# The tail of a fused attention and spectral-mixing kernel: order, PSUM banks and pieces of the last rows

## The chip, the cores and the metric

The kernel runs on one NeuronCore of a Trainium2 chip. The metric is device time in microseconds from one execution, and a kernel's time is the median of its runs; less is better. Before the change three runs gave 427.49, 428.01 and 428.20 us, so the median is 428.01 us.

A core has five engines with instruction streams of their own: TensorE (PE in the profile; its weight loads are listed as PEld), VectorE (DVE), ScalarE (ACT), GpSimd (POOL) and SyncE (SP). They meet only through semaphores. Sixteen DMA engines move data between HBM and SBUF; SP, ACT and POOL each put transfers into a queue of their own. TensorE writes its results to PSUM, which has 8 banks of 512 float32 columns by 128 partitions. ACT and DVE read PSUM and write SBUF.

## The reference

Inputs q, k, v have the shape (8, 8, 576, 64): batch, heads, sequence, head width. Four heads attend to the last 32 positions and four to positions at a stride of 32. The result is laid out as x with shape (8, 576, 512). Then a spectral layer follows:

```
X = rfft(x, axis=1)[:, :64]                 # 64 modes
Yr = Xr @ w_r - Xi @ w_i                    # per mode: 512 x 512 matrices
Yi = Xr @ w_i + Xi @ w_r
u  = x + irfft(Y)                           # Y is zero above mode 63
out = u + max(u @ w_ch, 0)                  # w_ch is 512 x 512; out is (8, 576, 512) float32
```

The weights w_r and w_i are 64 x 512 x 512 float32 each (134 MB together) and are read once. The output is 9.44 MB.

## The kernel before

The work runs in stages: attention per batch; a discrete Fourier transform by matmul; the products with the mode weights; and the way back. A mode's weights are loaded in two halves of the 512 input channels (`ORDER`), by POOL, which casts them to float16 on the way. The load order sets the order of the modes. The last to come are modes 48 to 63 of half 0, which are slot 1 of the function `mode`; the very last four are loaded one mode at a time, real and imaginary part in a DMA each (line 190).

`mode(1, m)` for these modes multiplies with the weights as the stationary operand: 16 matmuls of 16 columns (line 630). Eight modes share one PSUM bank `y`. `spectrum` (DVE, line 563) then adds the half that was computed before and writes the whole spectrum `YT`. For modes 56 to 63 it is called twice, after mode 61 for six modes and after mode 63 for two.

The inverse transform of 64 modes is split in groups of 16 modes. The sum is linear, so the kernel also carries u @ w_ch through the spectrum: z = Y @ w_ch per mode (`spec_z`, line 736, four matmuls accumulating over channels), and y turned by four transposes. The first three groups are added early (`renew`) to `v0` (rows of x @ w_ch) and `xo` (rows of x), both kept in float16. The last group, modes 48 to 63, is the tail's work. z and y of it come in two halves of the batch: `zzs[0]`, `yys[0]` for batches 0 to 3, `zzs[1]`, `yys[1]` for batches 4 to 7.

The tail has 18 items. An item is a pair of batches and one of four row blocks of 128 rows (items 0 to 15, of which 0 to 7 are batches 0 to 3), or four batches and their last 64 rows (items 16 and 17, t = 4). For each item k:

- `v_early(k)` puts v0 into a PSUM pair of two banks (two matmuls of 512 columns with an identity, line 987). `new_rows(k, v, zzs)` adds the last group (two to four matmuls with 32 rows, line 1001). `v_done(k)` is the relu on ACT (line 1013).
- `u_early(k)` and `new_rows(k, u, yys)` do the same with xo (lines 992, 1001). `u_done(k)` adds u and the relu on DVE into `osb` (line 1020), and SP issues the store (line 1028). For t = 4 the store goes as four DMAs of 64 rows (line 1031), two from SP and two from ACT; batches of even number lie on partitions 0 to 63, those of odd number on 64 to 127.

`pieces(k)` says whether ACT, DVE and the store take an item whole or as two batches after each other.

The order of instructions on each engine is the order in which the Python program issues them (`manual_schedule`), and each engine works it off in order. Tile pools hand out buffers and put in the waits that reuse needs. In the tail, PSUM pool `p` has three pairs, pool `y` two single banks; after the last mode `y` is closed, its two banks become `zp` and `yp` (pool `s`), and after that the one pair `u`. Whoever takes `u` first must wait until both `zp` and `yp` have been read.

Before the change the sequence is: modes 56 to 61 with `renew` between them; mode 62; `v_early(0)`, `v_early(1)`, `u_early(0)`; mode 63; z of the first half; one copy by ACT; eight transposes for both halves of y; two copies by DVE; items 0 and 1; then a loop in which v of item k and u of item k - 1 go side by side. z of the second half is computed at k = 8, in a bank of pool `p`:

```
        if k == 8:
            held = psum("p", pair=True)[:, 0]
            spec_z(3, 1, held)
            act_copy(zzs[1], held)
```

Of the kernel before, what the change touches and what calls it, by code (L numbers as in the profile page):

```python
# [10 lines left out]
FP = mybir.dt.float32  # L11
# [8 lines left out]
NM = 64  # L20
# [36 lines left out]
def kernel(  # L57
# [10 lines left out]
    nc = tc.nc  # L68
# [6 lines left out]
    pss = {}  # L75
# [10 lines left out]
    def psum(kind, half=False, pair=False):  # L86
        if pair:
            return pss[kind].tile([128, 2, 512], FP, tag=kind, name=kind)
        if half:
            return pss[kind].tile([128, 1024], F16, tag=kind, name=kind)  # L90
        return pss[kind].tile([128, 512], FP, tag=kind, name=kind)
# [28 lines left out]
    YS = {}  # L120
# [33 lines left out]
    w_chs = {}  # L154
# [95 lines left out]
    def act_copy(out, in_):  # L250
        nc.scalar.activation(out=out, in_=in_, func=ACTF.Copy)  # L251
# [303 lines left out]
    def flush():  # L555
        while queued:
            queued.pop()()
# [56 lines left out]
    def mode(slot, m):  # L614
        half = 1 - slot
        if m % 2:
            flush()
        if slot == 0 or m < SPLIT0:
            if m % 2:
                mode_pair(slot, m - 1)  # L620
            return
        mi, mg = m % 8, m // 8
        if mi == 0:
            ypt[slot] = psum("y")
        yp = ypt[slot]
        yv = yp.rearrange("p (m e x) -> p m e x", m=8, e=4)
        wt = w_tiles[ORDER.index((half, m))]
        for e in range(4):
            for c in range(4):
                nc.tensor.matmul(  # L630
                    yv[:, mi, e, :],
                    wt[:, XC[c], ds(128 * e, 128)],
                    Xh[half][:, c, :, :, m],
                    start=(c == 0),
                    stop=(c == 3),
                )
        if m % 2:
            w_fetch()
        ends = {5: 6, 7: 2} if mg == 7 else {7: 8}
        if mi in ends:  # L640
            n = ends[mi]
            m0 = mi + 1 - n
            spectrum(
                slot,
                (slice(None), slice(None), mg // 2, slice(None), ds(8 * (mg % 2) + m0, n)),
                yp.rearrange("p (m e x) -> p e x m", m=8, e=4)[:, :, :, ds(m0, n)],
            )
# [85 lines left out]
    def spec_z(g, bq, zp):  # L733
        for e in range(4):
            lhs = YS["YT"][:, e, g, ds(8 * bq, 8), :].rearrange("p x m -> p (x m)")
            nc.tensor.matmul(
                zp, lhs, w_chs["n"][:, e, :], start=(e == 0), stop=(e == 3)
            )
# [102 lines left out]
    for b in range(B):  # L841
# [12 lines left out]
        n = 0  # L854
        nm = NMODES[b]
        for mi in range(nm):
# [3 lines left out]
            n = upto  # L860
# [8 lines left out]
    zzs = [ptr.tile([128, DM], F16, name=f"zz{i}") for i in range(B)]  # L869
    yys = [ptr.tile([128, DM], F16, name=f"yy{i}") for i in range(B)]  # L870
# [56 lines left out]
    n = 0  # L927
    for m in range(SPLIT0):
# [4 lines left out]
        n = upto  # L933
# [33 lines left out]
    for n, i in enumerate([3, 5, 7] + list(range(8, 21))):  # L967
        b, t = n // 2, n % 2 * 2
# [8 lines left out]
    LAST = len(items) - 1  # L977
    vps, ups, rls, osbs = {}, {}, {}, {}
# [3 lines left out]
        return [kept[b][:, t] for b in bs] if t < 4 else [half[b // 2] for b in bs[::2]]  # L982

    def v_early(k):
        vps[k] = psum("p", pair=True)
        for j, r in enumerate(own(items[k], v0s, v0h)):
            nc.tensor.matmul(vps[k][:, j], idn, r, start=True, stop=False)  # L987

    def u_early(k):
        ups[k] = psum(("p", "u")[k % 2], pair=True)  # L990
        for j, r in enumerate(own(items[k], xos, xoh)):
            nc.tensor.matmul(ups[k][:, j], idn, r, start=True, stop=False)

    def new_rows(k, acc, spectra):
        bs, t = items[k]
        for j, b in enumerate(bs):
            q = ds(32 * (b % 4), 32)
            o, cols = acc[:, j % 2], out_cols(t)
            if t == 4:
                o = acc[ds(64 * (b % 2), 64), j // 2]  # L1000
            nc.tensor.matmul(  # L1001
                o, A3[q, cols], spectra[b // 4][q], start=False, stop=True
            )

    def pieces(k):
        return [slice(0, 1), slice(1, 2)] if k == 0 else [slice(0, 2)]

    def v_done(k):
        rl = ptr.tile([128, 2, 576], FP, tag=("xT", "rl")[k // 2 % 2], bufs=2, name="rl")
        rls[k] = rl[:, :, 0:DM]  # L1010
        vp = vps.pop(k)
        for j in pieces(k):
            nc.scalar.activation(out=rls[k][:, j], in_=vp[:, j], func=ACTF.Relu)  # L1013

    def u_done(k):
        bs, t = items[k]
        up, rl = ups.pop(k), rls.pop(k)
        osb = pw.tile([128, 2, DM], FP, tag="w", name="osb")
        for j in pieces(k):
            nc.vector.tensor_tensor(  # L1020
                out=osb[:, j], in0=up[:, j], in1=rl[:, j], op=AluOp.add
            )
            if t < 4:
                rows = out[:, ds(128 * (t - t % 2), 256), :].rearrange(
                    "b (p i) e -> p b i e", i=2
                )
                own_b = slice(bs[0] + j.start, bs[0] + j.stop)
                nc.sync.dma_start(rows[:, own_b, t % 2], osb[:, j])
        if t == 4:
            for b in bs:  # L1030
                (nc.scalar if b % 2 else nc.sync).dma_start(
                    out[b, ds(512, 64), :], osb[ds(64 * (b % 2), 64), b // 2 % 2, :]
                )

    flush()
# [5 lines left out]
            w()  # L1041
    yctx.close()
    with tc.tile_pool(name="ps_s", bufs=1, space=PSUM) as pss["s"]:
        zp = pss["s"].tile([128, 512], FP, name="zp")
        yp = pss["s"].tile([128, 2, 512], F16, name="yp")
        spec_z(3, 0, zp)
        act_copy(zzs[0], zp)
        for bq in range(2):
            for e in range(4):
                lhs = YS["YT"][:, e, 3, ds(8 * bq, 8), :].rearrange("p x m -> p (x m)")  # L1050
                nc.tensor.transpose(yp[:, bq, ds(128 * e, 128)], lhs, idn)
        for bq in range(2):
            nc.vector.tensor_copy(out=yys[bq], in_=yp[:, bq])
    pss["u"] = pctx.enter_context(tc.tile_pool(name="ps_u", bufs=1, space=PSUM))

    for k in range(2):
        new_rows(k, vps[k], zzs)
    for k in range(2):
        v_done(k)
    for k in range(2):  # L1060
        if k:
            u_early(k)
        new_rows(k, ups[k], yys)
        u_done(k)
    for k in range(2, LAST + 2):
        if k == 8:
            held = psum("p", pair=True)[:, 0]
            spec_z(3, 1, held)
            act_copy(zzs[1], held)
        if k <= LAST:  # L1070
            v_early(k)
        if k > 2:
            u_early(k - 1)
        if k <= LAST:
            new_rows(k, vps[k], zzs)
        if k > 2:
            new_rows(k - 1, ups[k - 1], yys)
        if k <= LAST:
            v_done(k)
        if k > 2:  # L1080
            u_done(k - 1)
    psum_pools()


# [28 lines left out]
```

## Time and profile before

The page does not give the profiled execution's whole time; its span is 426.7 us, 1.3 us under the median of the three runs.

| What | Value |
|---|---|
| Median of three runs | 428.01 us |
| Span of the profiled execution | 426.7 us |
| PE, DVE, ACT busy | 346.4, 234.7, 218.3 us |
| Last weight DMA issued, time to its landing | 382.31 us, 9.6 us |
| First store issued | 396.88 us |
| Stores of items 0 to 15 | 17 DMAs, 343 to 392 ns of SP each, 2.1 to 3.8 us to landing |
| Stores of items 16 and 17 | 8 DMAs of 128 KB, 528 to 846 ns of the issuer each, 2.4 to 3.4 us to landing |
| DMA share, 410.2 to 420.0 us | 1.02, 379 GB/s |

How to read it: a row of the timeline has the start, the duration, engine, line, operation and tiles, and in brackets the idle time of the engine before it and what ended it. A row of the windows has, for a stretch of time, each engine's busy time, the granted clock of TensorE as a share of full speed, the mean busy share of the 16 DMA engines and what they moved. A share slightly over 1 comes from packets that overlap.

### The profile page before, as it was taken

The numbers are of one execution on the slowest core, as the hardware profiler recorded it, in microseconds if no ns is written. First come the engines' busy times: TensorE is split into PE (matmuls) and PEld (weight loads), VectorE is DVE, ScalarE is ACT, GpSimd is POOL, SyncE is SP. The second block draws the span as 40 slices with busy tenths as digits, with TensorE's granted clock in tenths as the row PEclk, the third lists the DMA queues.
The fourth block names the chain that finished last, engine by engine and source line by source line (L and its number), as shares of the span: only waits on it lengthen the run. The fifth ranks groups of instructions, "written<-read, shape, count | busy, mean of one in ns | idle before, by whom it ended". The sixth has DMA issues, their size and how long they took to land.

```text
span 426.7 us, 9768 instructions
## 1 busy us (share of the span) xinstructions
PE 346.4 (81%) x4167; PEld 208.2 (49%) x4167; DVE 234.7 (55%) x466; ACT 218.3 (51%) x390; POOL 110.7 (26%) x196
## 2 busy tenths in 40 slices
PE   2977878769999698889768788878788867889993
PEld 2866767554656365566433344435444423445330
DVE  3788778851355154356113246746676354655884
ACT  1687678643656356556642235423442444443872
POOL 8332333322423222222222322222232222210000
PEclk9999899967999689999995889989999979989997
DMA  8999999999999999999999999999999999995698
GB/s 150 210 212 212 213 213 213 211 211 211 214 213 213 213 213 215 212 214 215 210 214 211 213 214 213 210 213 215 212 213 214 213 213 214 214 212 105 244 355 287
DMA packets 30938, 91.62 MB, mean 215 GB/s; under 512 B 4464, under 2 KB 5232, under 8 KB 30896
## 3 DMA queue, kind: packets, MB, share of 16 engines
q0 software_dynamic: 25168, 81.28, 96.2%
q1 hardware_dynamic: 4976, 9.13, 5.9%
q10 hardware_dynamic: 752, 0.61, 0.5%
q8 instruction: 32, 0.52, 0.5%
q14 instruction: 10, 0.08, 0.0%
HBM read 162.83 MB, written 9.44 MB: 404 GB/s over the span
## 4 chain that ended last, share of the span: by engine, by line
DMA 47%; PE 29%; DVE 14%; ACT 5%; issue 3%; DVEq 0%; POOL 0%; ACTq 0%; POOLq 0%
DMA wt<-in_moe_w_i_dram 38%; DMA wt<-in_moe_w_r_dram 7%; PE y L597 5%; DVE xb L241 3%; DVE kz L283 3%; PE p L987 2%; ACT X L251 2%; PE sc L532 2%; PE tp L413 2%; PE sc L459 1%; PE p L1001 1%; PE y L532 1%; PE p L760 1%; DVE yy L752 1%; DVE rec L240 1%
## 5 line engine op out<-in xcount | busy, mean ns | idle before, releaser
L597 PE MATMUL y<-wt,X 128*32 128x512 f16 (+1 forms) x448 | 70.9, 430 | 20.1 <-DMA wt<-in_moe_w_i_dram 20.1
L186 POOL DMA_DIRECT2D wt<-in_moe_w_r_dram x59 | 34.7, 588 | 126.4 <-PE y L597 56.3
L186 POOL DMA_DIRECT2D wt<-in_moe_w_i_dram x60 | 35.4, 590 | 68.3 <-DMA wt<-in_moe_w_i_dram 44.4
L597 PEld LDWEIGHTS <-X 128*32 128x32 f16 (+1 forms) x448 | 28.1, 140 | 39.4 <-DMA wt<-in_moe_w_i_dram 18.6
L727 DVE COPY xo<-tp 128x512 f16<-128x512 f16 x32 | 22.1, 691 | 36.8 <-PE tp L725 36.8
L726 ACT ACTIVATE v<-sc 128x512 f16<-128x512 f32 x32 | 19.1, 597 | 44.2 <-PE sc L717 44.2
L717 PE MATMUL sc<-w_cp,xT 128*128 128x512 f16 x128 | 36.9, 410 | 1.9 <-DVE xT L690 1.9
L489 ACT ACTIVATE PL<-sc 128x480 f16<-128x480 f32 (+1 forms) x48 | 27.0, 578 | 21.3 <-PE sc L475 21.0
L241 DVE TENSOR_TENSOR xb<-av,rec 90x256 f16<-90x256 f32 (+2 forms) x80 | 36.0, 450 | 2.8
L240 DVE RECIPROCAL rec<-av 90x4 f32<-90x4 f32 (+2 forms) x80 | 14.6, 183 | 39.3 <-PE av L504 28.2
L251 ACT ACTIVATE yr<-y 128x512 f16<-128x512 f32 x28 | 16.7, 597 | 36.8 <-PE y L597 35.6
L961 DVE TENSOR_TENSOR xo<-p,xo 128x1024 f16<-128x1024 f32 x16 | 19.6, 1225 | 21.7 <-PE p L760 21.7
L420 DVE COPY qT<-tp 128x576 f16<-128x576 f16 x16 | 11.9, 752 | 34.7 <-PE tp L413 34.7
L251 ACT ACTIVATE v<-p 128x1024 f16<-128x1024 f32 x16 | 16.4, 1023 | 23.1 <-PE p L760 23.1
L378 ACT ACTIVATE PL<-sc 90x360 f16<-90x360 f32 (+1 forms) x48 | 22.7, 490 | 7.0 <-PE sc L371 6.4
L251 ACT ACTIVATE v<-tp 128x640 f16<-128x640 f16 (+1 forms) x24 | 19.0, 807 | 11.8 <-PE tp L447 9.3
L413 PE MATMUL tp<-cI_s,ring 64*64 64x64 f16 x864 | 22.4, 197 | 2.7 <-DVE qT L420 2.4
L459 PE MATMUL sc<-cMl_s,cI_s 128*128 128x480 f16 (+1 forms) x48 | 19.4, 405 | 4.5 <-ACT PL L489 2.9
L276 PE MATMUL tp<-cI_s,ring 72*128 72x72 f16 x256 | 15.4, 207 | 8.7 <-DMA ring<-in_v_dram 7.1
L413 PEld LDWEIGHTS <-ring 64*64 64x64 f16 x864 | 17.5, 110 | 9.4 <-issue 5.4
L251 ACT ACTIVATE kz<-tp 64x360 f16<-64x360 f16 (+1 forms) x32 | 18.9, 592 | 6.2 <-PE tp L413 5.2
L1013 ACT ACTIVATE rl<-p 128x1024 f32<-128x1024 f32 (+1 forms) x19 | 18.4, 979 | 5.7 <-PE p L1001 3.1
(142 smaller groups left out, 737.9 us busy)
## 6 DMA issues: line engine op xcount, KB each, us to landing
wt<-in_moe_w_i_dram POOLq DMA_DIRECT2D x60, 512.0 KB, 18.8
wt<-in_moe_w_r_dram POOLq DMA_DIRECT2D x59, 512.0 KB, 17.7
out_dram<-osb SPq DMA_DIRECT2D x15, 512.0 KB, 3.4
ring<-in_v_dram POOLq DMA_DIRECT2D x8, 288.0 KB, 13.4
ring<-in_q_dram POOLq DMA_DIRECT2D x8, 288.0 KB, 13.6
ring<-in_k_dram POOLq DMA_DIRECT2D x8, 288.0 KB, 13.1
ring<-in_v_dram POOLq DMA_DIRECT2D x3, 512.0 KB, 14.8
ring<-in_q_dram POOLq DMA_DIRECT2D x3, 512.0 KB, 14.8
```

Of the source, the lines that this page charges most:

```text
L186: nc.gpsimd.dma_start(dst, rows)
L241: nc.vector.tensor_tensor(out=dst, in0=val.rearrange("p h (q c) -> p h c q", c=4), in1=rec[0:n, 0:pieces] .to_broadcast((n, pieces, 64)) . ...
L251: nc.scalar.activation(out=out, in_=in_, func=ACTF.Copy)
L378: nc.scalar.activation(out=PS[0:n, ds(POFF[t], 4 * n)], in_=scp[0:n, 0 : 4 * n], func=ACTF.Exp, scale=SCALE,)
L413: nc.tensor.transpose(tp[ds(64 * hp, 64), ds(64 * i, 64)], qn[ds(64 * hp, 64), ds(64 * (9 * g + i), 64)], idn[ds(64 * hp, 64), ds(64 * hp, ...
L459: nc.tensor.matmul(scp[:, 0 : n * times].rearrange("p (h x) -> p h x", h=times), idn, mask_rows("cMl", n, times), start=True, stop=False,)
L489: nc.scalar.activation(out=dst, in_=src, func=ACTF.Exp, scale=SCALE)
L597: nc.tensor.matmul(yp[ds(a, 32), :], Xh[half][pr, c].rearrange("p b r (h m) -> p (b r h) m", h=2)[:, :, mm % 32], wt[pr, XC[c], :], start= ...
L717: nc.tensor.matmul(vp, xT[:, ch], w_chs["cp"][:, ch, :], start=(ch == 0), stop=(ch == 3),)
L726: nc.scalar.activation(out=v0, in_=vp, func=ACTF.Copy)
L727: nc.vector.tensor_copy(out=xo.rearrange("p (h q c) -> p h q c", h=2, c=4), in_=tp[:, 0:512].rearrange("p (h c q) -> p h q c", h=2, c=4),)
L961: nc.vector.tensor_tensor(out=xo, in0=up[:, 0:n], in1=xo, op=AluOp.add)
```

## The change

It has six parts, all in the last 36 us.

1. Modes 62 and 63 get a PSUM bank `y` of their own, so mode 62 no longer writes to the bank that the spectrum of modes 56 to 61 is read from.
2. z is computed in two column halves of 256 (eight matmuls instead of four), and ACT copies each half by itself.
3. The second half's z and y move from item 8 (z) and from before item 0 (y) to just behind item 0. `u_early(1)` now takes pool `p`, and the pair `u` holds v of the even items from 2 on, where before it held u of the odd ones.
4. Item 2 is done alone, v and then u; item 3's v comes alone; from item 4 on the loop runs as before.
5. ACT works on items 0, 1 and 2 in halves, DVE and the stores on items 0, 1, 2, 3 and the last (17).
6. The stores of items 16 and 17 go as six DMAs instead of eight: two of 256 KB for item 16, both from SP, and four of 128 KB for item 17, of which ACT issues the two of partitions 64 to 127.

```diff
-        if mi == 0:
+        if mi == 0 or m == NM - 2:
             ypt[slot] = psum("y")
...
     def v_early(k):
-        vps[k] = psum("p", pair=True)
+        vps[k] = psum("p" if k < 2 or k % 2 else "u", pair=True)
...
     def u_early(k):
-        ups[k] = psum(("p", "u")[k % 2], pair=True)
+        ups[k] = psum("p", pair=True)
...
-    def pieces(k):
-        return [slice(0, 1), slice(1, 2)] if k == 0 else [slice(0, 2)]
+    def pieces(k, cut):
+        return [slice(0, 1), slice(1, 2)] if k in cut else [slice(0, 2)]
...
     def v_done(k):
-        for j in pieces(k):
+        for j in pieces(k, (0, 1, 2)):
             nc.scalar.activation(out=rls[k][:, j], in_=vp[:, j], func=ACTF.Relu)
     def u_done(k):
-        for j in pieces(k):
+        for j in pieces(k, (0, 1, 2, 3, LAST)):
...
-        if t == 4:
-            for b in bs:
-                (nc.scalar if b % 2 else nc.sync).dma_start(
-                    out[b, ds(512, 64), :], osb[ds(64 * (b % 2), 64), b // 2 % 2, :]
+                continue
+            for h in range(2):
+                own_b = slice(bs[0] + h + 2 * j.start, bs[0] + 2 * j.stop, 2)
+                (nc.scalar if h and k == LAST else nc.sync).dma_start(
+                    out[own_b, ds(512, 64), :].rearrange("b p e -> p b e"),
+                    osb[ds(64 * h, 64), j],
                 )
...
-        zp = pss["s"].tile([128, 512], FP, name="zp")
         yp = pss["s"].tile([128, 2, 512], F16, name="yp")
-        spec_z(3, 0, zp)
-        act_copy(zzs[0], zp)
-        for bq in range(2):
+
+        def last_z(bq):
+            zp = pss["s"].tile([128, 512], FP, name="zp")
+            parts = [ds(256 * h, 256) for h in range(2)]
+            for part in parts:
+                for e in range(4):
+                    lhs = YS["YT"][:, e, 3, ds(8 * bq, 8), :].rearrange(
+                        "p x m -> p (x m)"
+                    )
+                    nc.tensor.matmul(
+                        zp[:, part],
+                        lhs,
+                        w_chs["n"][:, e, part],
+                        start=(e == 0),
+                        stop=(e == 3),
+                    )
+            for part in parts:
+                act_copy(zzs[bq][:, part], zp[:, part])
+
+        def last_y(bq):
             for e in range(4):
                 lhs = YS["YT"][:, e, 3, ds(8 * bq, 8), :].rearrange("p x m -> p (x m)")
                 nc.tensor.transpose(yp[:, bq, ds(128 * e, 128)], lhs, idn)
-        for bq in range(2):
             nc.vector.tensor_copy(out=yys[bq], in_=yp[:, bq])
+
+        last_z(0)
+        last_y(0)
+        new_rows(0, vps[0], zzs)
+        new_rows(1, vps[1], zzs)
+        v_done(0)
+        new_rows(0, ups[0], yys)
+        u_done(0)
+        last_y(1)
+        last_z(1)
     pss["u"] = pctx.enter_context(tc.tile_pool(name="ps_u", bufs=1, space=PSUM))
 
-    for k in range(2):
-        new_rows(k, vps[k], zzs)
-    for k in range(2):
-        v_done(k)
-    for k in range(2):
-        if k:
-            u_early(k)
-        new_rows(k, ups[k], yys)
-        u_done(k)
+    v_done(1)
+    u_early(1)
+    new_rows(1, ups[1], yys)
+    u_done(1)
     for k in range(2, LAST + 2):
-        if k == 8:
-            held = psum("p", pair=True)[:, 0]
-            spec_z(3, 1, held)
-            act_copy(zzs[1], held)
+        us = {2: [2], 3: []}.get(k, [k - 1])
         if k <= LAST:
             v_early(k)
-        if k > 2:
-            u_early(k - 1)
-        if k <= LAST:
+            if k == 2:
+                new_rows(k, vps[k], zzs)
+                v_done(k)
+        for i in us:
+            u_early(i)
+        if 2 < k <= LAST:
             new_rows(k, vps[k], zzs)
-        if k > 2:
-            new_rows(k - 1, ups[k - 1], yys)
-        if k <= LAST:
+        for i in us:
+            new_rows(i, ups[i], yys)
+        if 2 < k <= LAST:
             v_done(k)
-        if k > 2:
-            u_done(k - 1)
+        for i in us:
+            u_done(i)
```

## The prediction

> **What bounds the kernel now.** I read the page's 40 slices first, then the busy time by windows over the last 36 us, the timeline of the same stretch, and the DMA issues.
>
> ```profile
> span 426.7 us, 9768 instructions
> ...
> DMA  8999999999999999999999999999999999995698
> ```
>
> Each digit is a slice of 10.7 us. For 36 slices the DMA engines are full with weights and inputs; the change touches nothing there. It touches the last four slices (5, 6, 9, 8): the gap between the last weights and the first store, then the stores.
>
> ```profile
> core 0: us, PE busy (x) PEld busy (x) DVE busy (x) ACT busy (x) POOL busy (x), PEclk, DMA share, GB/s
> ...
> 399.10:399.70 0.60, 0.60 (x4) 0.19 (x2) 0.60 (x1) 0.60 (x1) 0.00 (x0) 1.00 0.20 55
> ...
> 408.10:408.80 0.70, 0.70 (x8) 0.16 (x6) 0.70 (x1) 0.70 (x1) 0.00 (x0) 1.00 0.11 38
> 408.80:421.20 12.40, 10.89 (x73) 3.31 (x72) 11.29 (x10) 8.32 (x9) 0.00 (x0) 1.00 1.01 377
> 421.40:421.90 0.50, 0.00 (x0) 0.00 (x0) 0.00 (x0) 0.00 (x0) 0.00 (x0) 1.00 1.01 209
> 422.00:423.20 1.20, 0.00 (x0) 0.00 (x0) 0.00 (x0) 0.00 (x0) 0.00 (x0) 0.50 0.95 326
> ```
>
> These say what the tail waits for. From 408.8 to 421.2 the DMA share is 1.01 at 377 GB/s: items 7 to 15, nine stores of 512 KB, leave in 12.4 us, 1.38 us each. PE makes an item every 1.295 us (store issues at 409.26, 410.56, 411.86). So the stores, not TensorE, pace the tail, and **only idle DMA time and slow DMA time can be won or lost there**. There are two idle gaps: 0.6 us at 399.1, and 0.7 us at 408.1, where the second z (`held`) holds PE and the next store is issued at 407.97 instead of 406.8. The slow stretch is the end: at 421.4 the engines are as full as before, yet move 209 GB/s.
>
> ```profile
> 389.93 0.10 PEld L630 LDWEIGHTS <-wt 128*128 128x128 f16 x1 [0.39 <-issue]
> ...
> 390.54 0.64 PE L630 MATMUL y<-X,wt 128*128 128x16 f16 x16 [0.53 <-DVE YT L563]
> ...
> 392.31 0.64 PE L630 MATMUL y<-X,wt 128*128 128x16 f16 x16
> ...
> 393.33 1.04 PE L736 MATMUL zp<-w_ch,YT 128*128 128x512 f16 x4 [0.39 <-DVE YT L563]
> ...
> 394.45 0.60 ACT L251 ACTIVATE zz<-zp 128x512 f16<-128x512 f32 x1 [4.03 <-PE zp L736]
> ...
> 395.10 0.40 PE L1001 MATMUL p<-zz,cFl_s 32*128 32x512 f16 x4 [0.29 <-ACT zz L251]
> ```
>
> This is the chain to the first store: mode 62 (held 0.53 us by the spectrum that reads its bank), mode 63, the last spectrum, z, its copy, the first item's rows; the store is issued at 396.88. All times below are on this profile's clock.
>
> **Part 1, modes 62 and 63 in a bank of their own.** The 0.53 us wait goes: mode 62 starts at about 389.97. What is late next is the weight of mode 63. Its last load is issued at 382.31 and takes 9.6 us, so it lands at 391.9; after the landing at 377.1 the matmul started at 377.24. So mode 63 starts at about 392.09 instead of 392.31. Gain 0.22 us; ends 0 and 0.53.
>
> **Part 2, z by halves.** PE streams the same columns (four of 512 or eight of 256), no change. A half copy on ACT is estimated from 597 ns for 512 columns and 1023 ns for 1024: 597 - 213 = 384 ns, two make 0.77 us, less some 0.1 us of overlap (four relus in a row, 3.24 us by their sum, take 3.11). A gain needs the first copy to run beside the second four matmuls. But in the built program the first copy waits for PE and the second for nothing: both stand behind the eighth matmul. Loss 0.1 us; ends -0.2 (overlap after all) and +0.17. With part 1 the first rows start at 394.98 and the first store goes out at 396.76, 0.12 us sooner.
>
> **Part 3, the second z in front.** What PE no longer does at 404.05 is worth 2.46 - 1.30 = 1.16 us of cadence (issues at 405.51 and 407.97). What it does instead, in order, after the first u rows at 395.21 (0.33): four transposes (0.22, from 0.61 for eight), z (0.86, four times 216 ns), then `u_early(1)` at 396.62 and its rows until 397.48. `v_early(2)` now takes the bank pair of z and yp, so it waits for both readers. ACT's half copies (z ends 396.8) stand behind the two relus of item 0 and end at about 397.55. DVE's copy of yy1 stands behind both halves of item 0: 396.04 + 2 x 0.69, less 0.1, then 0.42, makes 397.72. That wait costs 0.24 us. Queued behind these copies are relu 1 on ACT and the first half of item 1 on DVE.
>
> Then the matmuls that were merged stand apart. Merged, the four short row matmuls of v and u share one slot (v_early 0.44, u_early 0.53, rows 0.33: the 1.295). Apart, a v or u with its rows costs 0.86. Items 2 and 3 now go v2, u2, v3 apart: 397.72 + 3 x 0.86 = 400.30 for `v_early(4)`; before it was 398.87. It has 1.43 us of delay, of which 1.16 comes back at item 7. The u rows of item 3 follow at 401.27, those of item 4 at 402.56.
>
> Stores, by DVE (0.69 a half, 1.22 whole) and 0.02 to the issue: item 0 at 396.76 and 397.35; item 1 at 398.78 and 399.35 (before: 398.82 whole); item 2 at 400.21 and 400.80 (400.32 whole); item 3 at 402.38 and 402.98 (401.62 whole); item 4 at 404.21 (402.92). The two halves cost DVE 0.15 us per item, beside PE's slots from item 4 on. Packets start 0.85 us after an issue into an idle queue (407.97 to the end of the gap at 408.8). Served at 0.69 us a half, the engines idle before items 1, 3 and 4: about 0.65, 0.8 and 0.45 us. Item 4's packets start at 405.06. From there twelve items at 1.38 us end at 421.6; before, item 15 ended at 421.2. **Loss 0.4 us.** Ends: -0.4, if half stores fill the gaps and item 4 is ready by 403.5; +0.8, if another of the waits counted here as hidden shows.
>
> **Part 4, the end.** The same 1.05 MB in six stores instead of eight. Issuing: item 16's two stores are both SP's (0.56 us each); item 17's first half goes out 0.6 us sooner, its four stores from 420.9, the last issued at about 422.4 instead of 422.9. All are queued before the engines are through, so issue time costs nothing; if the engines did wait for issues, it would gain 0.5 us.
>
> What they find is the slow stretch. A 64-row store reads partitions 0 to 63 or 64 to 127. At 421.4 only SP's stores of the lower half were moving: 209 GB/s. From 422.0 SP's lower and ACT's upper ones mixed: 326. In all 1.05 MB took 421.2 to 425.1, 3.9 us. Now SP holds, in order, 262 KB lower, 262 KB upper, then 2 x 131 KB lower; ACT holds 2 x 131 KB, all upper. So: lower alone until ACT's arrive (0.65 us at 209, 0.136 MB); the mix (0.26 MB at 326: 0.8 us); SP's upper beside ACT's upper (0.39 MB at 209: 1.9 us); the lower rest alone (0.26 MB at 209: 1.25 us). Sum 4.6 us, **loss 0.7 us**. Ends: 2.8 us (all at 377, -1.1) and 5.0 us (all at 209, +1.1). I take the worked order, the only one built from rows of 64-row stores.
>
> The Trainium skill bears on this against the change. SBUF - State Buffer, section "Can I just issue two DMAs to hit both halves?", says that two transfers on opposite 64-partition halves serialize, since each half reaches only 8 of 16 ports. This trace agrees for one queue (209 GB/s) and not for two (326). By the rule as it stands the end would take 5.0 us whatever the order, a sum of 429.5; by the rows it is 4.6.
>
> **Sum.** 426.7 + 0.4 + 0.7 = 427.8 us of span. The median of the three runs shown, 428.0, stands 1.3 us above this span, for what lies around it; that stays. **Forecast 429.0 us.** A difference under 0.2% (0.86 us) is about what a measurement of this kernel cannot tell from none.
>
> **Rivals.**
> *The end as before.* Engines read ahead across queues, so long one-sided runs don't matter; the 326 row speaks for it, the 209 row against. Only part 3 is left: 428.4. If item 4 is ready sooner too, 428.0.
> *Faster.* The stores end at the full 377 GB/s (-1.1), or the gaps are filled by the half stores (-0.4 in place of +0.4): 427.3 with the first alone, 426.5 with both. It decides if the last 1.05 MB take under 3.0 us. For it: fewer stores, issued sooner. Against it: no 64-row store here has run at 377.
> *Slower still.* ACT's stores come so late that nothing mixes (end 5.0 us), or one more wait in front (+0.8): 429.5 to 429.9.
>
> **How the numbers follow.** Forecast 0.40 (own range 428.6 to 429.4), the end as before 0.25, faster 0.17, slower still 0.18. Slower by over 0.2% (above 428.87): 0.18 and three quarters of the forecast's case, 0.48. Faster (below 427.15): most of the third case, 0.14. Within: 0.38. Leaving out a tenth on each side gives 427.1 to 429.9.
>
> **What the changed profile would show.** Mode 62 without its DVE wait and mode 63 at 0.2 us after the last landing; two half copies back to back, the first starting only after the eighth z matmul; `v_early(2)` waiting for DVE's yy copy; item 4's store issued about 1.3 us later than before, item 7's within 0.2 us; no gap at 408 and one at 402 to 405; over 1 us of the end with a DMA share near 1 and about 210 GB/s. I am wrong if item 4 is stored before 403.5, or if the last 1.05 MB take under 4.0 us.

## The result and the profile after

The changed kernel takes 429.38 us (median of 16 runs, 428.37 to 430.96); the kernel before took 427.79 us (16 runs) in the same comparison. The ratio is 1.0035, with a 95% interval of 1.0025 to 1.0045: **slower by 1.5 us** (1.1 to 1.9). The forecast was 429.0.

The two pages alone would hide this: the span after is 426.8 us and before 426.7. The executions profiled differ ahead of the change. The last weight landed at 391.21 us in the profile after (issued at 381.59, 9.62 us to landing) and at 391.94 before. So times below count from that landing, which nothing in the change can move: that load is issued before the first changed instruction. The profile after is of one of the faster of its 16 runs (428.54 us). In every run here with a span on record the time is at least 1.7 us more than the span; by that, the execution profiled before took about 428.4 us or more (an estimate), and was one of the slower ones.

The page after, the DMA row of the 40 slices:

```profile
span 426.8 us, 9802 instructions
...
DMA  8999999999999999999999999999999999995698
```

It is the same row as before, digit for digit; slices of 10.7 us are too coarse. Busy time by windows shows the difference (stretch, its length, engines' busy time, granted clock, DMA share, GB/s):

```profile
core 0: us, PE busy (x) PEld busy (x) DVE busy (x) ACT busy (x) POOL busy (x), PEclk, DMA share, GB/s
398.20:398.80 0.60, 0.60 (x5) 0.16 (x4) 0.32 (x1) 0.60 (x2) 0.00 (x0) 1.00 0.23 68
400.20:400.70 0.50, 0.50 (x7) 0.10 (x4) 0.00 (x0) 0.50 (x1) 0.00 (x0) 1.00 0.15 53
402.10:402.60 0.50, 0.50 (x6) 0.21 (x3) 0.49 (x2) 0.31 (x1) 0.00 (x0) 1.00 0.06 21
404.10:404.60 0.50, 0.50 (x6) 0.10 (x4) 0.50 (x1) 0.50 (x1) 0.00 (x0) 1.00 0.08 29
405.40:421.00 15.60, 13.85 (x90) 4.16 (x88) 14.25 (x13) 10.81 (x11) 0.00 (x0) 1.00 1.02 378
421.30:422.10 0.80, 0.00 (x0) 0.00 (x0) 0.00 (x0) 0.00 (x0) 0.00 (x0) 1.00 0.98 202
422.40:424.90 2.50, 0.00 (x0) 0.00 (x0) 0.00 (x0) 0.00 (x0) 0.00 (x0) 0.74 0.95 277
```

The first four rows are gaps: stretches in which the DMA engines are mostly idle. Before, there were two, at 399.1 and at 408.1. The one at 408.1 is gone, and four stand in front where there was one. In all four PE is busy for the whole window: the rows to be stored are still being made. From 405.4 on the stores run at 378 GB/s, the same rate as the 377 before, so nothing of what the gaps cost can come back. Then comes the end. It is one-sided at first, which means that only stores of one half of the partitions move, at 202 GB/s, and then runs at 277 GB/s, where before 326 were seen.

The chain to the first store, from the timeline after (start, duration, engine, line, operation, tiles, idle time before it and what ended it):

```profile
388.92 0.64 PE L630 MATMUL y<-X,wt 128*128 128x16 f16 x16 [0.72 <-DMA wt<-in_moe_w_i_dram]
...
391.35 0.64 PE L630 MATMUL y<-X,wt 128*128 128x16 f16 x16 [0.49 <-DMA wt<-in_moe_w_i_dram]
...
392.37 1.05 PE L1056 MATMUL zp<-w_ch,YT 128*128 128x256 f16 x8 [0.39 <-DVE YT L563]
...
393.50 0.66 ACT L251 ACTIVATE zz<-zp 128x256 f16<-128x256 f32 x2 [4.89 <-PE zp L1056]
...
394.21 0.40 PE L1001 MATMUL p<-zz,cFl_s 32*128 32x512 f16 x4 [0.57 <-ACT zz L251]
```

Mode 62 waits for its weights, no longer for the spectrum. The two half copies of z start at 393.50, when all eight matmuls (392.37 + 1.05) are through, and take 0.66 us where the one copy took 0.60. And the wait in front of item 2, in the same view:

```profile
396.47 0.41 DVE L1070 COPY yy<-yp 128x512 f16<-128x512 f16 x1
...
397.03 0.59 PE L987 MATMUL u<-v,cI_s 128*128 128x512 f16 x2 [0.26 <-DVE yy L1070]
```

`v_early(2)`, now in the pair `u`, waits 0.26 us for DVE's copy of the second y.

### The profile page after: what moved, and what is told of

It is laid out like the page before. It is cut to its first block, busy times and chain, and to the rows that moved or that the text cites. A ratio compares the mean times of both kernels' runs of the same rounds, so it can differ in the third digit from the quotient of the medians.

```text
span 426.8 us, 9802 instructions
## 1 busy us (share of the span) xinstructions
PE 342.2 (80%) x4175; PEld 207.5 (49%) x4175; DVE 235.0 (55%) x470; ACT 218.6 (51%) x394; POOL 111.0 (26%) x196
## 4 chain that ended last, share of the span: by engine, by line
DMA 47%; PE 21%; DVE 5%; ACT 2%; issue 2%; POOL 0%; DVEq 0%; ACTq 0%; POOLq 0%
DMA wt<-in_moe_w_i_dram 35%; DMA wt<-in_moe_w_r_dram 12%; PE y L597 5%; PE p L992 2%; PE tp L413 1%; PE y L532 1%; ACT X L251 1%; DVE yy L752 1%; PE sc L459 1%; PE u L987 1%; PE p L987 1%; PE sc L717 1%; PE p L1001 1%; PE sc L475 1%; DVE xb L241 1%
## 5 line engine op out<-in xcount | busy, mean ns | idle before, releaser
L597 PE MATMUL y<-wt,X 128*32 128x512 f16 (+1 forms) x448 | 68.9, 419 | 21.8 <-DMA wt<-in_moe_w_i_dram 21.5
L1020 DVE TENSOR_TENSOR osb<-p,rl 128x1024 f32<-128x1024 f32 (+1 forms) x23 | 22.3, 990 | 4.2 <-ACT rl L1013 2.8
```

Source lines behind the costliest of these rows:

```text
L597: nc.tensor.matmul(yp[ds(a, 32), :], Xh[half][pr, c].rearrange("p b r (h m) -> p (b r h) m", h=2)[:, :, mm % 32], wt[pr, XC[c], :], start= ...
L1020: nc.vector.tensor_tensor(out=osb[:, j], in0=up[:, j], in1=rl[:, j], op=AluOp.add)
```

## The experiments

One table first, for all kernels but three (the short rows sooner and the two of full width, whose items or end cannot be compared in these columns; they stand below). All columns are us after the landing of the last weight, in one profiled execution each: the issue of the first store, of item 4's and of item 7's; the moment when 1.5 MiB of output are left, worked out from the DMA packets of the trace (it lies in the stores of 128 rows, shortly before the end begins); and the landing of the last store. "End" is the difference of the last two columns.

| Kernel | first | item 4 | item 7 | 1.5 MiB left | last landing | end | ratio to before, 95% |
|---|---|---|---|---|---|---|---|
| before | 4.94 | 10.97 | 16.03 | 28.13 | 33.63 | 5.50 | 1 |
| after | 4.78 | 12.44 | 16.32 | 28.69 | 34.58 | 5.89 | 1.0035 (1.0025 to 1.0045) |
| after, end undone | 4.78 | 12.44 | 16.32 | 28.71 | 34.26 | 5.55 | 1.0026 (1.0014 to 1.0038) |
| end alone | 4.71 | 10.74 | 15.80 | 27.89 | 34.05 | 6.16 | 1.0022 (1.0010 to 1.0033) |
| bank alone | 4.70 | 10.74 | 15.79 | 27.88 | 33.54 | 5.66 | 0.9992 (0.9983 to 1.0001) |
| after, order undone | 4.78 | 10.88 | 15.98 | 28.05 | 34.17 | 6.12 | 1.0014 (1.0005 to 1.0023) |
| after, halves undone | 4.71 | 12.29 | 16.18 | 28.60 | 34.67 | 6.07 | 1.0029 (1.0018 to 1.0041) |
| end by two sides | 4.70 | 10.74 | 15.79 | 27.88 | 33.88 | 6.00 | 1.0007 (0.9995 to 1.0020) |
| after, side by side | 4.78 | 12.01 | 15.90 | 28.36 | 34.27 | 5.91 | 1.0022 (1.0010 to 1.0035) |
| end in short stores | 4.71 | 10.74 | 15.80 | 27.89 | 33.43 | 5.54 | 1.0007 (0.9995 to 1.0019) |
| best of the parts | 4.71 | 10.74 | 15.80 | 27.87 | 33.27 | 5.40 | 1.0004 (0.9995 to 1.0014) |

Single profiles scatter. Before, end undone and bank alone have the same stores at the end, and it took 5.50, 5.55 and 5.66 us. End alone, order undone, after, halves undone and side by side share another end, and it took 5.89 to 6.16 us. So a difference of 0.2 us between two ends says nothing by itself.

The theory after the result was that of the prediction: order and end each cost, the bank gives a little. The rivals were that one of the two costs all, or that the parts do not add. The edits are shown shortened: three dots stand for lines left out.

**The end undone.** The changed kernel with the eight stores of before:

```diff
-            for h in range(2):
-                own_b = slice(bs[0] + h + 2 * j.start, bs[0] + 2 * j.stop, 2)
-                (nc.scalar if h and k == LAST else nc.sync).dma_start(...)
+        if t == 4:
+            for b in bs:
+                (nc.scalar if b % 2 else nc.sync).dma_start(...)
...
-        for j in pieces(k, (0, 1, 2, 3, LAST)):
+        for j in pieces(k, (0, 1, 2, 3)):
```

> The changed kernel with the old stores of items 16 and 17 (eight of 128 KB, SP the lower and ACT the upper 64 partitions, item 17 whole). Theory: the order of one-sided stores costs 0.4 us (item 15's landing to the last landing took 3.7 us before, 4.1 after) to the 0.7 us predicted, so this kernel stands 0.4 to 0.7 us under the changed one, about 0.9 us over the one before, and the last stretch is 3.7 us again. Rival, the front alone is the loss: no difference to the changed kernel within 0.2 us.

Measured: 428.84 us, 1.0026. The front is as in the changed kernel to 0.02 us; the end is 0.34 us shorter. The time is 0.4 us under the changed kernel's by the ratios, but the two intervals overlap.

**The end alone.** The kernel before with the six stores of the change, item 17 in halves.

```diff
-        if t == 4:
-            for b in bs:
-                (nc.scalar if b % 2 else nc.sync).dma_start(...)
+            for h in range(2):
+                (nc.scalar if h and k == LAST else nc.sync).dma_start(...)
```

> The kernel before with only the end changed: six stores for items 16 and 17, SP both sides of item 16, item 17 in halves. Theory: 0.4 to 0.7 us slower than before, a DMA share near 1 at about 210 GB/s for over 1 us of the end. Rival, fewer and earlier stores help by themselves: up to 0.5 us faster, as the last issue goes out that much sooner.

Measured: 428.71 us, 1.0022: 0.9 us by itself. The end took 6.16 us against 5.50. So the end costs, and the front is not needed for that.

**The bank alone.**

```diff
-        if mi == 0:
+        if mi == 0 or m == NM - 2:
```

> The kernel before with modes 62 and 63 in a PSUM bank of their own, nothing else. Theory: mode 63 waits for its weights instead, so 0.2 us faster (0.53 if the weights did not matter), first store 4.7 us after the last weight's landing instead of 4.94. Rival: the 0.2 us only lengthens the idle gap at item 8, the time is the same.

Measured: 427.39 us, 0.9992; the interval reaches from a gain of 0.7 us to a loss of 0.04. The profiles say more than this time. Four other kernels here keep the old bank and are the same as before up to the end. Mode 62 and 63 in the one with the end alone:

```profile
388.95 0.64 PE L630 MATMUL y<-X,wt 128*128 128x16 f16 x16 [1.31 <-DMA wt<-in_moe_w_i_dram]
...
391.37 0.31 PE L630 MATMUL y<-X,wt 128*128 128x16 f16 x5 [0.48 <-DMA wt<-in_moe_w_i_dram]
```

Mode 62 waits for its weights there too, and the first store goes out 4.70 or 4.71 us after the last landing in all four, exactly as with the bank. The wait of 0.53 us for the spectrum, on which part 1 was reckoned, stood in the profiled execution of before and in none of these four. In four of five executions with the old bank there was nothing to remove.

In the execution profiled with the bank alone there was something. PE came late to mode 62, as in the profile of before:

```profile
390.38 0.55 DVE L563 TENSOR_TENSOR YT<-y,Y 128x384 f16<-128x384 f32 x1
390.38 0.65 PE L630 MATMUL y<-X,wt 128*128 128x16 f16 x16
...
392.34 0.64 PE L630 MATMUL y<-X,wt 128*128 128x16 f16 x16
```

Mode 62 runs beside the spectrum, where in before it started only when the spectrum was through (389.94 + 0.55, then 390.54). The last weight landed at 392.20 here, and mode 63 starts 0.14 us later, against 0.37 us later in before. So the bank does what part 1 says in such an execution. Of the 14 profiled executions two are of this sort, before and this one; in the other 12 mode 62 waits for its weights.

**The order undone.** The changed kernel's bank, halves and end on the order of before, with the second z at k = 8 again (the edit against the kernel before; the lines of z's halves and of the six stores are left out).

```diff
+        if mi == 0 or m == NM - 2:
...
+        for j in pieces(k, (0, 1, 2)):
...
+        for j in pieces(k, (0, 1, 2, 3, LAST)):
```

> The changed kernel with the old order of the tail: both turns of y in front, second z at item 8, v and u of neighbouring items side by side, pools as before; bank, z halves of the first z, halves of items 0 to 3 and 17, and the six stores stay. Theory: the new order costs about 0.4 us net (1.3 us of delay at item 4, 1.16 given back at item 8, the rest by the DMA engines having no slack), so this one is 0.3 to 0.6 us faster than the changed kernel, with a gap of 0.5 to 0.8 us before item 7's store. Rival, the halves are what costs: no faster than the changed kernel.

Measured: 428.36 us, 1.0014, so 0.9 us under the changed kernel. The two intervals do not overlap. With 1.5 MiB left it is 0.64 us ahead of the changed kernel, and 0.41 us at the last landing. The order costs at the front, and most of that is never given back.

**The halves undone.** The changed kernel with z whole, and items 1 to 3 whole.

```diff
-        for j in pieces(k, (0, 1, 2)):
+        for j in pieces(k, (0,)):
...
-        for j in pieces(k, (0, 1, 2, 3, LAST)):
+        for j in pieces(k, (0, LAST)):
...
+            spec_z(3, bq, zp)
+            act_copy(zzs[bq], zp)
```

> The changed kernel, with z whole again (four matmuls of 512 columns, one copy) and items 1 to 3 whole again on ACT, DVE and in the stores; the new order, the bank and the new end stay. My theory: the halves neither fill the gaps nor cost much (z's halves 0.1 us, DVE's halves 0.15 us an item beside other work); the time is that of the changed kernel less 0.1 us, about 429.3, and item 4's store stays within 0.3 us of 12.4 us after the last weight's landing. Rival: the halves do fill gaps under the new order, and without them the idle DMA time grows by 0.4 us or more: 429.8 or above. Second rival: the halves are the cost of the new order, because relu 1, DVE's copy of yy1 and v_early(2) stand behind them: item 4 is stored 0.5 us sooner or more, and the time is about 428.8.

Measured: 428.75 us, 1.0029, not to be told from the changed kernel. The first store is 0.07 us sooner (z's halves), item 4 is 0.15 sooner. Its gaps:

```profile
398.50:400.00 1.50, 1.50 (x8) 0.41 (x8) 1.30 (x2) 0.86 (x2) 0.00 (x0) 1.00 0.07 18
402.80:403.40 0.60, 0.60 (x7) 0.16 (x5) 0.60 (x1) 0.60 (x1) 0.00 (x0) 1.00 0.05 14
```

These two are together as long as the four of the changed kernel, 2.1 us: the halves only cut the gaps into smaller ones. From the first store's issue until 1.5 MiB are left, the DMA share is 0.90 over 23.9 us in both kernels. The first rival falls. The second named about the time that came (428.8), but not its way: item 4 was to be stored 0.5 us sooner or more.

**Side by side.** The changed kernel with items 2 and 3 in the loop as before; the second z stays in front.

```diff
-        us = {2: [2], 3: []}.get(k, [k - 1])
+        us = [k - 1] if k > 2 else []
```

> The changed kernel, but items 2 and 3 go side by side again (v of item k with u of item k - 1 from item 3 on), while the second z stays in front. My theory: the delay of item 4 is two parts, the second z in front (about 1 us, with the wait of v_early(2)) and the parting of items 2 and 3 (two times 0.86 less 1.3 = 0.43 us); so item 4's store comes 0.4 us sooner, 12.0 us after the last weight's landing, item 7's as well, and the time falls by 0.3 to 0.4 us to about 429.0. Rival: the parting costs nothing, because the stores of items 1 to 3 in halves feed the DMA engines meanwhile, and without it item 2's store comes later: 429.4 or above.

Measured: 428.50 us, 1.0022. Item 4's store comes 0.43 us sooner, item 7's 0.42, as expected, and 0.33 us of it are still there when 1.5 MiB are left. What remains of the delay at item 7, against the kernels with the old order, is 0.11 us, 0.07 of it from z's halves. So in PE's time the second z in front is paid back at item 7 almost whole, as it only changes its place, while the parting of items 2 and 3 adds 0.43 us (two slots of 0.86 us in place of one of 1.30) that is never paid back. In the time of the stores the second z is not paid back whole: with 1.5 MiB left this kernel is still 0.31 us behind the one with the order undone (28.36 against 28.05), and 0.10 us at the last landing. The ratios, 1.0022 and 1.0014, cannot tell the two apart. The windows of this kernel, the last gap and the stretch after it:

```profile
403.70:404.20 0.50, 0.50 (x7) 0.08 (x4) 0.50 (x1) 0.50 (x1) 0.00 (x0) 1.00 0.14 49
405.00:420.60 15.60, 13.92 (x91) 4.16 (x88) 14.32 (x13) 10.86 (x11) 0.00 (x0) 1.00 1.02 377
```

After the last gap the stores again run at 377 GB/s; the gap just ends 0.4 us sooner (both landings lie within 0.1 us of each other on this clock).

**What makes the end slow.** First, SP with the lower and ACT with the upper partitions, for both items; the number and size of the stores are those of the end alone, against which the edit is shown.

```diff
-                (nc.scalar if h and k == LAST else nc.sync).dma_start(
+                (nc.scalar if h else nc.sync).dma_start(
```

> The kernel before, with six stores at the end as in the change, but SP takes the lower 64 partitions and ACT the upper ones for both items, so the two sides always stand in different queues. The number, size and pieces of the stores are those of the end alone, which came to 1.0022 of the kernel before; only item 16's upper store moves from SP to ACT. My theory: the long one-sided runs cost, not the number of stores; the last landing is 3.7 to 3.9 us behind item 15's as before the change, and the ratio is 1.000, at most 1.001. Rival: the larger or fewer stores, or the halves of item 17, cost as such: 4.3 us and 1.002.

Measured: 428.37 us, 1.0007, and an end of 6.00 us. The ratio is as expected, and lower than the end alone's 1.0022, though the intervals overlap. In the profile the end is hardly shorter, so the expectation missed there. Its windows:

```profile
420.50:421.80 1.30, 0.00 (x0) 0.00 (x0) 0.07 (x1) 0.00 (x0) 0.00 (x0) 1.00 0.85 180
421.80:424.80 3.00, 0.00 (x0) 0.00 (x0) 0.00 (x0) 0.00 (x0) 0.00 (x0) 0.74 0.92 277
```

ACT's upper store is issued at the same time as SP's lower one (419.40). Still the engines spend 1.3 us at 180 GB/s, and in that time only packets of SP's queue move; ACT's first packet starts at 422.1. That leaves the size of the stores as what could lengthen the end. Next, then, item 16 in four stores of 128 KB instead of two of 256 KB, nothing else (the edit against the run just shown):

```diff
-            for h in range(2):
-                own_b = slice(bs[0] + h + 2 * j.start, bs[0] + 2 * j.stop, 2)
-                (nc.scalar if h else nc.sync).dma_start(...)
+            for b in range(bs[0] + 2 * j.start, bs[0] + 2 * j.stop):
+                (nc.scalar if b % 2 else nc.sync).dma_start(...)
```

> The kernel before with its eight stores of 128 KB at the end, lower ones from SP and upper ones from ACT in turn, and only item 17 in halves on DVE. It differs from the run with SP lower and ACT upper in the size of item 16's stores alone (four of 128 KB instead of two of 256 KB). My theory after that run, where 0.26 MB left one-sided at 180 to 205 GB/s before ACT's first packet moved: the engines work a store off before they turn to the other queue, so the one-sided stretch is as long as the first store, and stores of 128 KB halve it; the last landing is 3.7 us behind item 15's and the ratio is 1.000. Rival: the halves of item 17 cost, not the size: 4.2 us and 1.001 to 1.002.

```profile
420.40:421.20 0.80, 0.00 (x0) 0.00 (x0) 0.08 (x1) 0.00 (x0) 0.00 (x0) 0.57 0.92 210
421.20:424.20 3.00, 0.00 (x0) 0.00 (x0) 0.00 (x0) 0.00 (x0) 0.00 (x0) 0.50 0.88 300
```

The slow start is 0.8 us instead of 1.3, and the end 5.54 us, as before. The last landing is 3.70 us behind item 15's, as expected. In both kernels ACT's packets set in as SP's first store runs out: 1.8 us after the issue here (419.31, first packet at 421.1), 2.7 us in the run above (419.40, 422.1). So a longer first store went with a longer one-sided stretch. That is what the two profiles show. The times of the two kernels (427.95 and 428.37 us, both 1.0007) cannot tell them apart, so a price of the size in device time is not shown.

The row of 300 GB/s also speaks against the rule weighed in the prediction. The Trainium skill, SBUF - State Buffer, section "Can I just issue two DMAs to hit both halves?", says that two transfers on opposite halves serialize, measured at 6% over a single one. Here they ran together at 300 GB/s over 3.0 us, against 180 to 210 one-sided. What the runs here share with the rule is that one half alone is slow.

**Short rows sooner.** The kernel before with the bank, the 64-row items as the 9th and 16th, SP with the lower and ACT with the upper side.

```diff
-    items += [(range(b, b + 4), 4) for b in (0, 4)]
+    items.insert(8, (range(0, 4), 4))
+    items.insert(15, (range(4, 8), 4))
...
-        if k == 8:
+        if k == 9:
```

> The kernel before with the bank for modes 62 and 63 and another order of items: the two items of 64 rows are the 9th and the 16th instead of the last two, SP storing their lower and ACT their upper partitions, and the second z stands one item later. The last two items are now ones of 128 rows. My theory: 64-row stores are slow only where nothing of 128 rows is beside them, so the last 1.05 MB leave at 377 GB/s in 2.8 us instead of 3.7, and with the bank's 0.3 us the time is 426.6 to 426.9, ratio 0.997. Rival: a 64-row store takes its time wherever it stands, so only the bank's gain is left: 427.4, ratio 0.999.

Measured: 430.29 us, 1.0056 (1.0044 to 1.0068): neither the theory nor the rival. Its windows, before, during and after the first 64-row item, and the end:

```profile
409.20:410.40 1.20, 1.19 (x8) 0.38 (x7) 1.17 (x1) 0.41 (x1) 0.00 (x0) 1.00 0.05 17
410.60:413.50 2.90, 2.43 (x16) 0.80 (x15) 2.17 (x2) 2.32 (x3) 0.00 (x0) 1.00 1.00 241
413.70:420.30 6.60, 6.51 (x44) 2.08 (x40) 5.57 (x6) 4.10 (x4) 0.00 (x0) 1.00 1.04 394
421.00:422.30 1.30, 0.00 (x0) 0.00 (x0) 0.86 (x1) 0.40 (x1) 0.00 (x0) 1.00 0.95 225
422.30:424.00 1.70, 0.00 (x0) 0.00 (x0) 0.36 (x1) 0.00 (x0) 0.00 (x0) 1.00 0.97 281
424.00:425.40 1.40, 0.00 (x0) 0.00 (x0) 0.00 (x0) 0.00 (x0) 0.00 (x0) 0.54 1.06 408
```

The very end does run at 408 GB/s. But a 64-row item costs its slow stretch wherever it stands (241 GB/s over 2.9 us in the middle, 225 and 281 later), the gap at the second z grew to 1.2 us, and ACT's issues (0.73 and 0.64 us) now stand between relus that are still needed.

**Full width.** The kernel before with the last two items in four stores over all 128 partitions, all from SP; a second kernel adds the bank and item 17 in halves.

```diff
+            for i in range(j.start, j.stop):
+                nc.sync.dma_start(
+                    out[bs[0] + 2 * i : bs[0] + 2 * i + 2, ds(512, 64), :], osb[:, i]
+                )
```

> The kernel before, and only the stores of items 16 and 17 changed: each takes 64 rows of two batches, so all 128 partitions, 256 KB; four stores, all from SP. My theory: what makes the end slow is that a store reads only one half of the partitions; a store that reads both moves at the 377 GB/s of the other items. The last 1.05 MB then take about 2.8 us of DMA time instead of 3.7, and the ratio is 0.998 (about 0.9 us less). Rival: stores of 64 rows are slow for another reason (their size, their place in HBM, the issue times of SP), so one queue alone without ACT's share is no faster: 1.000, or 1.002 as with the stores of the change.

> The full-width end of the run above, with the bank for modes 62 and 63 and item 17 in halves (ACT whole, DVE and the store in two pieces, so its first 256 KB are issued about 0.6 us sooner); the order stays as before the change. My theory: the gains add, 0.9 us from the end and 0.3 us from the bank, and the halves let the last bytes queue without a gap: ratio 0.997, about 426.6. Rival: with the end no longer slow, the last issue (30.4 us after the last weight's landing) decides, and what is won at the front is not seen: 0.998 or above.

Measured: 445.74 us, 1.0410 (1.0396 to 1.0425), and 445.95 us, 1.0421. Windows of the first:

```profile
425.00:430.00 5.00, 0.00 (x0) 0.00 (x0) 0.00 (x0) 0.00 (x0) 0.00 (x0) 0.50 0.13 51
430.00:435.00 5.00, 0.00 (x0) 0.00 (x0) 0.00 (x0) 0.00 (x0) 0.00 (x0) 0.50 0.13 51
```

A DMA share of 0.13 is what two busy engines of sixteen would give; the trace does not say which engines ran. The store goes to two batches of 64 rows, so the outermost size of its pattern in HBM is 2. The Trainium skill, DMA: Bandwidth & Descriptors, section "Rules for kernel authors", says that an outermost dimension of fewer than 16 confines a transfer to at most so many engines; 2/16 = 0.125 agrees. The question that this run was for, whether a store of both sides at once would end the slow stretch, stays open. What the bank and item 17's halves add cannot be read from the second kernel either, as its end covers them. A pattern that has the 64 rows outermost was not tried.

**The best of the parts.** The bank, the eight stores of 128 KB, and items 16 and 17 in halves.

```diff
+        if mi == 0 or m == NM - 2:
...
+        for j in pieces(k, (0, LAST - 1, LAST)):
```

> The kernel before with the bank for modes 62 and 63, the eight stores of 128 KB in the old turn, and items 16 and 17 both in halves on DVE. ACT can issue item 16's first upper store when the relu of item 17 is through, about 0.2 us sooner than when DVE has the whole of item 16, and SP its first lower one about 0.5 us sooner. My theory: the end starts a little less one-sided and everything else is as before, so the gain is small, 0.2 us, and the bank gives none of its own where mode 62 waits for its weights anyway: ratio 0.9990 to 1.0000, no change that can be told. Rival: the one-sided stretch at the start of the end goes entirely, because both sides queue while item 15's store still moves: the last landing is 3.2 us behind item 15's and the ratio 0.998.

Measured: 427.81 us against 427.53, 1.0004 (0.9995 to 1.0014): no change that can be told, as the theory had it. Its last landing, 33.27 us, is the earliest of all, by 0.16 us over the short stores alone, which is within the scatter of single profiles. No kernel here beats the one before by more than the measurement can tell.

## Why the prediction was right, and where it was off

The direction and the mechanism held: the stores pace the tail, so only idle and slow DMA time counts, and the change adds to both. Undoing the order gives back 0.9 us, and the end alone costs 0.9 us, each clear of the noise. Of the measured 1.5 us the prediction named 1.0. By the profiles the changed kernel's last store lands 34.58 us after the last weight, and those of the two kernels with the old order, z whole and stores of 128 KB at the end (bank alone, end in short stores) at 33.54 and 33.43; that is 1.0 to 1.15 us, 0.8 of it there when 1.5 MiB are left. The spans say the same: the median of the changed kernel's 16 runs is 427.25 us, that of the kernel before in the first experiments' comparison (29 runs) 426.1. The rest of the 1.5 us lies in part outside the span, where the change has no instruction: time less span is 2.10 us in the mean in the changed kernel's runs, and 1.80 in those 29. No run here says why.

That the total came so close is partly luck. The front cost more than forecast and the end, in its place, less, and the two errors partly cancel. The median of before also came out 0.2 us lower over 16 runs than over the first three, which brought the forecast of 429.0 nearer to 429.38 than its difference of 1.0 us is to 1.5. The 1.3 us added to the span is not the time around it either: no run with a span on record shows less than 1.7. It set the median of three runs against the span of a slower execution, and did no harm, as it stands on both sides of the difference.

- **Part 1, a gain of 0.22 us: right for the execution it was read from, wrong for most.** The step took the 0.53 us wait of mode 62 as part of every execution. Four others with the old bank had no such wait, and there the first store goes out 4.70 to 4.71 us after the last landing, with or without the bank. For these the step's lower end, 0, was the right value. In the one with the bank alone PE came as late as in before, and the wait was gone: 4.70 us against 4.94. What the bank is worth in the median stays open: the interval of the bank alone, from a gain of 0.7 us to a loss of 0.04, holds both 0 and 0.22.
- **Part 2, a loss of 0.1 us: right.** The first store goes out at 4.78 us against 4.70 or 4.71, a loss of 0.07, by the mechanism named: both half copies stand behind the eighth matmul.
- **Part 3, the delay: right in its parts, 0.2 us short.** The wait of `v_early(2)` was put at 0.24 us and is 0.26. From the first store to item 4's it said 7.45 us; 7.66 were measured, against 6.03 before. At item 7 it left 0.25 us of delay (1.41 less 1.16); 0.45 are left (11.54 against 11.09). The 0.43 us of the parted items is what the run side by side gave back, 0.43 at item 4 and 0.42 at item 7. Idle gaps came before items 1, 2, 3 and 4 rather than 1, 3 and 4. In all the loss is 0.8 us when 1.5 MiB are left, against the kernels whose mode 62 waits for its weights, where the step had 0.4. One half of the difference is the missing gain of part 1, the other half these 0.2 us.
- **Part 4, a loss of 0.7 us: right by itself, apparently smaller in its place.** Alone, the end costs 0.9 us by time (0.4 to 1.4) and 0.66 by the profiles (6.16 against 5.50). Behind the new order it is 0.34 us (5.89 against 5.55) in the profiles and 0.4 in time, with intervals that overlap. With the scatter of single profiles, whether it really is smaller there is not shown. The worked order took sides for what matters. In the profiles, turning the sides around leaves an end of 6.00 us, and the short stores bring it to 5.54, which speaks for the size. By time, turning the sides alone brought 1.0022 to 1.0007, and the short stores brought nothing more. Which of the two the time goes by stays open.

The rival *the end as before* (428.4) falls by the end alone. *Faster* falls by the four gaps and by the 202 and 277 GB/s of the end. *Slower still* needed an end of 5.0 us, and the end was not that long. The two conditions that would have made the forecast wrong count on the clock of before: item 4's store before 403.5, which is 11.56 us after the last landing, and the last 1.05 MB under 4.0 us. Item 4 was at 12.44 us. From item 15's landing to the last one it took 4.10 us (3.70 before), so the second condition was not met, though only by a little.

## What to carry to other kernels

A wait seen in one profiled execution is not yet part of the kernel: where it depends on which of two arrivals comes last, look for it in a second execution before counting on its removal. Where stores pace a stage, work that is only moved is paid back in the issues when its old place comes, though the DMA time idled away before that is not all won back; work that was merged and is now done apart is not paid back at all. In the profiles here, stores of half the partitions ended soonest when short and in turn between two queues; six of them, with both sides of one item from one queue, cost 0.9 us. A store's outermost size is worth a look before its width.

## What was not expected of the hardware

Two queues with stores of opposite halves do not mix from the start: in the run by two sides ACT's store, issued with SP's at 419.40 us, moved its first packet only at 422.1, after a stretch of SP's packets alone at 180 GB/s. Four stores whose outermost size is 2 moved at 51 GB/s with a DMA share of 0.13, and cost 17.9 us together. And two profiles of kernels that differ by 1.5 us can show the same span, since the last weight landed 0.7 us apart in them.
